# The copy of the value sums ahead of both feature activations on the scalar engine

## Chip, cores and metric

The kernel runs on one core of one Trainium2 chip. The metric is the device time of one execution in microseconds (us); the median of several runs counts. The engines are named as in the profile: PE multiplies matrices, DVE is the vector engine, ACT the scalar engine, POOL the third elementwise engine, SP issues the transfers.

## What is computed

Four layers follow each other on x of 2048 rows by 512 in float32: A, B, A, B with the same weights each time. Each adds its result to x after a layer norm. The change lies in layer B, an attention with a memory, over 32 heads of width 16, in 4 segments of 512 rows:

```python
phi = lambda t: jnp.where(t > 0, t + 1.0, jnp.exp(t))
for s in range(N):
    qs, ks, vs = q[:, :, s], k[:, :, s], v[:, :, s]
    logits = jnp.einsum("bhqd,bhkd->bhqk", qs, ks) * scale + mask
    p = _softmax(logits, axis=-1)
    a_dot = jnp.einsum("bhqk,bhkd->bhqd", p, vs)
    pq = phi(qs)
    num = jnp.einsum("bhld,bhde->bhle", pq, M)
    den = jnp.einsum("bhld,bhd->bhl", pq, z)[..., None] + 1e-6
    a_mem = num / den
    o = g * a_mem + (1.0 - g) * a_dot
    outs.append(o)
    pk = phi(ks)
    M = M + jnp.einsum("bhld,bhle->bhde", pk, vs)
    z = z + jnp.einsum("bhld->bhd", pk)
```

Layer A (a linear attention with learned features) is not touched by the change.

## The kernel before

Layer B works on groups m = 0 to 31: a segment s = m // 8, a block c of 8 heads, and half of that block, 4 heads. The class LayerB writes the whole order of work by hand in `steps` (line 865). Its loop (line 941) runs over k, five steps for each group. Below, "step 5.2 of segment 0" means local group 5, third of its five steps (k = 8*5*s + 5*5 + 2). In each step stand, in this order:

- `attend` (line 776): products of keys and queries into lg, of which there is one buffer. ACT takes the exponential, lg to P; POOL zeroes the masked part of P.
- `maxima` (line 735), nine steps ahead of `attend`: the same products into the buffer mx for a later group. DVE takes row maxima out of it into mxs.
- what an earlier step put off: first the `late` list (DVE differences), then the `later` list.
- `weighted` (line 812), at steps .0 and .2: the product of P and the values into pv, one buffer. The sums of group m are finished at step .2 of group m + 1, and there ACT copies pv, scaled by share, into U (line 836). U has two buffers.
- the work of a table (GAPS, line 43, and LAST for the last segment): steps .1, .3 and .4 have a cell each, such as

```
5.1 max q1+~       | 5.3 fin v0+/3     | 5.4 v0+ t3
6.1 max a0+ k1+~   | 6.3 a0+ fin v1+/3 | 6.4 v1+ m3 load
7.1 max n n q2+~   | 7.3 fin n v2+/3   | 7.4 v2+ t0+
```

In the cells q, k and v are projections of queries, keys and values (a + means for the next segment), out is the output projection, a the product of a query's features with the memory, t and m the memory's update, n and ln pieces of the next layer norm, max the negated maxima, and fin is `finish` (line 839): PE transposes U of the group before, and DVE divides the sums by their row sum (`weigh`, line 366; buffers r, ot, wt or tmp).

A projection ends in `proj` (line 654). ACT writes the high part of the product pp (a buffer of g) into a buffer ta1 or U. DVE writes the low part, the difference, which a ~ in the cell puts off to the next step by `late`. If the features phi are needed, two functions go into `later` and run in the next step:

```python
def first():
    act.activation(e, pp, AF.Exp)

def second():
    act.activation(r, pp, AF.Relu)
    pool.tensor_scalar(e, e, 1.0, None, op0=MIN)
    pool.tensor_tensor(out=e, in0=e, in1=r, op=ADD)
```

The profile calls e and r both tb. Projections with features end at .1 of groups 0, 1, 2, 4, 5, 6 and 7 of a segment, so their two functions run at step .2, where `weighted` also writes U. One a segment (q0+) ends at 3.4 and its functions run at 4.0, where `weighted` only adds products to pv.

PE is held in the order of the program (`held`, line 125). From k = 3 on so are DVE, ACT and POOL in layer B (`Ordered`, line 107), except that the exponential of lg and the maxima have high priority. The buffers of g are three, used in turn; a product into g waits until the third one before it has been read by all its readers.

The scheduling loop and what it calls, with line numbers:

Of the kernel before, what the change touches and what calls it, by code (L numbers as in the profile page):

```python
# [69 lines left out]
def interleave_kernel(ctx, tc, x_in, a_wqkv, a_wphi, a_wo, b_wq, b_wk, b_wv, b_wo, b_beta,  # L70
# [109 lines left out]
    def load_w(key, src=None, tag="w8"):  # L180
        w = []
        for _ in bring(w, key, src, tag):
            pass
        return w
# [16 lines left out]
    def settle():  # L201
        for k, t in owed:
            dma(k, t)
        owed.clear()
# [10 lines left out]
    def plain(src):  # L215
        def get(kc):
            raw = T2("x", 4)
            nc.sync.dma_start(out=raw, in_=src[kc * P : (kc + 1) * P, :])
            return raw
        return get  # L220
# [194 lines left out]
    def chain(*gens):  # L415
        for g in gens:
            yield from g
# [37 lines left out]
    class LayerA:  # L455
# [4 lines left out]
        def pass1(self, first):  # L460
# [19 lines left out]
            for s in range(NSEG):  # L480
# [46 lines left out]
                def go(steps):  # L527
                    for step in steps.split():
                        yield from {"k": kproj, "q": qproj, "v": kv}[step[0]](int(step[1]))
                        if step == "q0" and s == NSEG - 1:  # L530
                            self.e0 = self.feats(0)
# [10 lines left out]
                for _ in go(steps):  # L542
                    n += SIDE
                    while n >= 1:
                        n -= 1
                        next(side, None)
                    yield
# [60 lines left out]
    class LayerB:  # L608
# [256 lines left out]
        def steps(self, side, after):  # L865

            N = 8 * NSEG
            at = chain(*[self.attend(m) for m in range(N)])  # L870
            ma = chain(*[self.maxima(m) for m in range(N)])
            self.w4 = []
            self.wnext = [(m, c) for _ in range(NSEG) for c in range(NC) for m in range(2)]
            norms = [self.norm(0)]
            for _ in range(6):
                next(norms[0])
            self.wv = load_w("bwv", plain(b_wv))
            settle()
            for _ in range(2):
                self.queue_w()  # L880
            mem = {(s, c): self.memory(s, c) for s in range(NSEG) for c in range(NC)}
            val = [self.values(s) for s in range(NSEG)]
            outs, proj, part = {}, {}, {}
            weights = self.weights()

            def do(what, s, k):
                self.put_off = what[-1] == "~"
                what, _, quarters = what.rstrip("~").partition("/")
                s += what[-1] == "+"
                what = what.rstrip("+")  # L890
                i = int(what[-1]) if what[-1].isdigit() else None
                op = what.rstrip("0123456789")
                if op == "max":
                    if (k + LEAD) // R <= N:
                        self.put_maxima((k + LEAD) // R - 1)
                elif op == "fin":
                    if k >= FINAT:
                        self.finish((k - FINAT) // R)
                elif op in ("q", "k", "v", "out"):
                    if op == "out":  # L900
                        if s == 0:
                            return
                        g = outs[s]
                    elif op == "v":
                        g = after if i is None else val[s]
                    else:
                        g = proj.setdefault((s, i, op), self.proj(s, i, "qk".index(op)))
                    n = int(quarters) if quarters else 4 - part.pop(op, 0)
                    if quarters:
                        part[op] = n  # L910
                    for _ in range(n):
                        next(g, None)
                elif op == "load":
                    if s < NSEG - 2:
                        norms.append(self.norm(s + 2 if k > 0 else 1))
                        next(norms[-1])
                elif op == "n":
                    if s != NSEG - 2 or k % (8 * R) < 6 * R:
                        next(after if s == NSEG - 1 else norms[-1], None)
                elif op == "ln":  # L920
                    next(after if s == NSEG - 1 else norms[-1], None)
                elif op in ("a", "t", "m"):
                    if op != "a" or s > 0:
                        next(mem[s, i], None)
                elif s > 0:
                    if s not in outs:
                        outs[s] = self.out(s - 1)
                    next(outs[s])

            table = {k: (v.split(), 0) for k, v in BEFORE.items()}  # L930
            for s in range(NSEG):
                for cell in (GAPS if s < NSEG - 1 else LAST).replace("|", "\n").split("\n"):
                    if cell.strip():
                        at_, *what = cell.split()
                        m, j = at_.split(".")
                        if s == 0:
                            what = [w for w in what if not w.startswith("v3")]
                        table[8 * R * s + R * int(m) + int(j)] = what, s
            slots = [k for k in range(BEGIN, 2) if k < -LEAD or k % R in FILL]
            spent = 0.0  # L940
            for k in range(BEGIN, R * N + 4):
                strict[0] = True
                m = k // R + 3
                if k % R == 0 and 0 <= m < N:
                    self.stack(m)
                if 0 <= k < R * N:
                    next(at)
                if -LEAD <= k < R * N - LEAD:
                    next(ma)
                ordered[0] = ORDERED <= k < R * N  # L950
                late, self.late = self.late, []
                for f in late:
                    f()
                later, self.later = self.later, []
                for f in later[:1]:
                    f()
                if k % R in (0, 2) and 0 <= k // R - 1 < N:
                    self.weighted(k // R - 1, k % R == 2)
                for f in later[1:]:
                    f()  # L960
                if k in slots:
                    want = LEFT * (1 + slots.index(k)) / len(slots) if k < slots[-1] else 1e9
                    while spent + 100 < want:
                        before = work[0]
                        if next(side, None) is PAUSE:
                            break
                        spent += work[0] - before
                what, s = table.get(k, ((), 0))
                for w in what:
                    do(w, s, k)  # L970
                if 18 <= k < 28 and k % R in FILL:
                    next(weights, None)
            self.finish(N - 1)
            self.put_off = False
            for _ in self.out(NSEG - 1):
                pass
            strict[0] = ordered[0] = False
# [52 lines left out]
```

## Time and profile before

| | |
|---|---|
| median of 3 runs | 1740.95 us (1740.75 to 1749.43) |
| profiled execution | 1744.38 us, span 1742.4 us |
| granted PE clock, mean | 0.961 |
| busy: PE, DVE, ACT, POOL | 1552.9, 1183.8, 785.7, 544.0 us |
| DMA, mean | 111 GB/s |

The span is the time from the first to the last instruction of the profiled execution, which itself took a little longer. Engines overlap, so the busy times don't add up. A row of the order of time holds the start in us, the duration in us, the engine, the line, the operation, what it writes and reads, and in brackets the idle time of the engine before it with what ended it. A row of the waits holds who waited for whom, the total in us, how often, and the longest. All operations of ACT, DVE and POOL bear line 116, and those of PE lines 137 and 141, since helpers issue them; the names of the buffers tell them apart.

The layer B's groups run from about 399 to 800 us and from about 1248 to 1640 us of the span, with some more behind each.

### The profile page before, as it was taken

How to read it: one execution, taken by the hardware profiler on the slowest of the kernel's cores; microseconds unless marked ns; L12 is line 12 of the kernel's file. 1: busy time of each engine (PE TensorE's matmuls, PEld its weight loads, DVE VectorE, ACT ScalarE, POOL GpSimd, SP SyncE). 2: the span in 40 equal slices, each digit the busy share in tenths (PEclk: the TensorE clock that was granted, in tenths of full speed). 3: DMA queues.
4: the chain of work that ended last, by engine and by line, in shares of the span. 5: the costliest groups of instructions: out<-in, count | busy, mean ns of one | idle time of the engine just before them, and what ended most of it. 6: DMA issues, size and time to landing. Idle time of an engine off the chain costs nothing.

```text
span 1742.4 us, 28146 instructions
## 1 busy us (share of the span) xinstructions
PE 1552.9 (89%) x9856; PEld 1105.5 (63%) x9856; DVE 1183.8 (68%) x3358; ACT 785.7 (45%) x1202; POOL 544.0 (31%) x840
## 2 busy tenths in 40 slices
PE   5999898978899999998889998888889999999987
PEld 4888787755555555654568887776555565565544
DVE  4666785567778778778546677745677777776761
ACT  5433343225555555555533333422455555545542
POOL 2322431212433443332221233120244434433321
PEclk9999999989999999999999998899799999999997
DMA  9512345323534334345232025333443343343310
GB/s 333 201 49 85 94 138 185 117 74 89 179 84 132 96 91 133 94 146 140 80 107 76 25 93 162 110 109 109 123 116 92 98 127 99 86 122 80 98 44 31
DMA packets 99973, 193.67 MB, mean 111 GB/s; under 512 B 13432, under 2 KB 27000, under 8 KB 96760
## 3 DMA queue, kind: packets, MB, share of 16 engines
q1 hardware_dynamic: 98680, 191.35, 37.3%
q8 instruction: 79, 1.29, 0.3%
q10 hardware_dynamic: 1152, 0.52, 0.1%
q14 instruction: 62, 0.51, 0.1%
HBM read 96.86 MB, written 41.94 MB: 80 GB/s over the span
## 4 chain that ended last, share of the span: by engine, by line
PE 64%; DVE 18%; ACT 7%; DMA 6%; issue 4%; SPq 1%; POOL 1%; DVEq 0%; ACTq 0%; POOLq 0%
PE g L137 40%; DVE mx L116 9%; PE mx L137 7%; PE lg L137 7%; PE pv L137 5%; PE g L141 4%; ACT P L116 2%; DMA x<-x 2%; DVE mxs L116 2%; ACT U L116 1%; DMA tb<-pq 1%; DVE st L116 1%; ACT tb L116 1%; ACT x L116 1%; DVE ta L116 1%
## 5 line engine op out<-in xcount | busy, mean ns | idle before, releaser
L116 DVE CUSTOM_DVE_ANT_0 mx<-mx,mask 128x128 f32<-128x128 f32 (+3 forms) x1024 | 511.0, 499 | 227.1 <-PE mx L137 193.3
L116 ACT ACTIVATE P<-lg 128x1024 f32<-128x1024 f32 x320 | 328.8, 1027 | 250.6 <-PE lg L137 247.5
L116 POOL TENSOR_SCALAR_AFFINE_SELECT P<-P 128x256 f32<-128x256 f32 (+1 forms) x448 | 191.0, 440 | 550.9 <-ACT P L116 550.8
L137 PE MATMUL mx<-e,e 63*128 63x256 f32 (+2 forms) x1024 | 158.4, 367 | 60.7 <-DVE mxs L116 53.0
L137 PE MATMUL g<-w,oh 128*128 128x512 f32 x512 | 181.8, 438 | 9.3 <-ACT oh L116 5.4
L137 PE MATMUL lg<-e,e 64*128 64x256 f32 (+2 forms) x1024 | 171.7, 393 | 15.6 <-ACT P L116 14.3
L137 PE MATMUL g<-hh,wqk 128*128 128x512 f32 x512 | 179.2, 409 | 1.5 <-ACT mt L116 1.5
L137 PE MATMUL pv<-P,v 128*32 128x512 f32 (+3 forms) x2048 | 171.3, 454 | 0.1
L137 PE MATMUL g<-w,hh 128*128 128x512 f32 x512 | 168.2, 409 | 0.5 <-DVE e L116 0.5
L137 PEld LDWEIGHTS mx<-e,e 63*128 63x128 f32 x1024 | 85.2, 191 | 113.3 <-DVE mxs L116 87.8
L137 PEld LDWEIGHTS lg<-e,e 64*128 64x128 f32 x1024 | 83.0, 188 | 112.5 <-issue 58.1
L116 DVE DVE_READ_ACCUMULATOR2_ANT mxs<- 128x1 f32 x1024 | 144.8, 141 | 0.0
L116 POOL TENSOR_SCALAR tb<-tb 128x512 f32<-128x512 f32 x48 | 71.3, 1486 | 184.6 <-ACT tb L116 184.6
L137 PEld LDWEIGHTS pv<-P,v 128*32 128x32 f32 x2048 | 54.9, 112 | 103.5 <-issue 90.5
L137 PEld LDWEIGHTS g<-w,oh 128*128 128x128 f32 x512 | 97.1, 205 | 33.2 <-ACT oh L116 7.3
L137 PEld LDWEIGHTS g<-hh,wqk 128*128 128x128 f32 x512 | 98.1, 192 | 23.8 <-ACT mt L116 2.5
L137 PE MATMUL g<-w,ol 128*128 128x512 f32 x256 | 107.6, 420 | 0.8 <-DVE ol L116 0.8
L137 PEld LDWEIGHTS g<-w,hh 128*128 128x128 f32 x512 | 92.1, 191 | 20.8 <-DVE e L116 0.7
L137 PE MATMUL g<-w,hl 128*128 128x512 f32 x256 | 101.1, 395 | 0.0
L137 PE MATMUL g<-hl,wqk 128*128 128x512 f32 x256 | 101.0, 395 | 0.0
L116 DVE TENSOR_REDUCE es<-P 128x64 f32<-128x1024 f32 x64 | 76.6, 1197 | 34.8 <-ACT P L116 34.7
L137 PE MATMUL g<-w,e 128*128 128x512 f32 x384 | 97.7, 396 | 0.0
(117 smaller groups left out, 2547.6 us busy)
## 6 DMA issues: line engine op xcount, KB each, us to landing
e<-ta SPq DMA_DIRECT2D x264, 128.0 KB
wqk<-wqk SPq DMA_DIRECT2D x64, 512.0 KB
x<-x SPq DMA_DIRECT2D x48, 256.0 KB
e<-U SPq DMA_DIRECT2D x80, 128.0 KB
pq<-tb SPq DMA_DIRECT2D x32, 256.0 KB
tb<-pq SPq DMA_DIRECT2D x32, 256.0 KB
xr<-x SPq DMA_DIRECT2D x29, 256.0 KB
x<-in SPq DMA_DIRECT2D x28, 256.0 KB
```

What stands on the lines that cost most here:

```text
L116: i = f(*a, **k)
L137: return held(nc.tensor.matmul(*a, **k))
L141: return held(nc.tensor.transpose(*a))
```

## The change

Before, the first function of `later` ran ahead of `weighted` and the others behind it. Now all run behind it. On ACT at step .2 the order was: exponential, copy to U, second activation. It becomes: copy to U, exponential, second activation. POOL's two operations on the features are still issued right behind the second activation.

```diff
                 late, self.late = self.late, []
                 for f in late:
                     f()
-                later, self.later = self.later, []
-                for f in later[:1]:
-                    f()
                 if k % R in (0, 2) and 0 <= k // R - 1 < N:
                     self.weighted(k // R - 1, k % R == 2)
-                for f in later[1:]:
+                later, self.later = self.later, []
+                for f in later:
                     f()
```

## Prediction

> **What bounds the kernel now.** I read the page first, then the waits of the matrix engine in the two stretches of layer B (399 to 800 us and 1248 to 1640 us of the span), then the order of time of three engines around single copies U. The page says that PE leads but is not alone.
>
> ```profile
> span 1742.4 us, 28146 instructions
> PE 64%; DVE 18%; ACT 7%; DMA 6%; issue 4%; SPq 1%; POOL 1%; DVEq 0%; ACTq 0%; POOLq 0%
> 399.00:800.00 401.00, 366.40 (x2608) 231.95 (x2606) 305.51 (x1037) 214.98 (x308) 154.91 (x264) 0.99 0.43 118
> PE g L141 <- ACT U L116: 16.8, 18, 1.2
> ```
>
> The second line gives the chain that ended last; the third is the stretch of the first layer B (length, then busy time of PE, weight loads, DVE, ACT and POOL, granted clock, DMA share, GB/s): PE busy 366 of 401 us at a clock of 0.99, so its instructions run at nearly full speed and only its idle time can be had. The fourth line is the largest wait of PE in that stretch, and the view for the second layer B answers with the same line: 18 times PE stood before the transposes of U until ACT had written U, 33.6 us in both layers. Single ones are of two sizes, 1.19 and 0.53 us (rows of both below); 11 and 7 of them make 16.8.
>
> What makes U late is the row of time at one of these places (step 5.2 of the first segment; ACT, then PE, then DVE):
>
> ```profile
> 460.89 0.60 ACT L116 ACTIVATE tb<-g 128x512 f32<-128x512 f32 x1 [1.28 <-DVE ta L116]
> 461.39 0.68 ACT L116 ACTIVATE U<-pv,share 128x512 f32<-128x512 f32 x1
> 461.96 0.60 ACT L116 ACTIVATE tb<-g 128x512 f32<-128x512 f32 x1
> 462.43 1.04 ACT L116 ACTIVATE P<-lg 128x1024 f32<-128x1024 f32 x1
> 458.65 1.28 PE L137 MATMUL pv<-P,v 128*32 128x384 f32 x16
> 460.37 0.56 PE L137 MATMUL mx<-e,e 63*128 63x256 f32 x4
> 462.12 0.66 PE L141 MATMUL g<-ident,U 128*128 128x128 f32 x4 [1.19 <-ACT U L116]
> 462.53 0.72 PE L137 MATMUL g<-w,hh 128*128 128x512 f32 x2
> 464.81 0.50 PE L137 MATMUL lg<-e,e 64*128 64x256 f32 x4
> 460.18 0.69 DVE L116 TENSOR_TENSOR ta<-g,ta 128x512 fp32r<-128x512 f32 x1
> 463.19 0.42 DVE L116 TENSOR_TENSOR ot<-g,r 128x256 f32<-128x256 f32 x1
> 465.58 0.43 DVE L116 CUSTOM_DVE_ANT_0 mx<-mx,mask 128x256 f32<-128x256 f32 x1 [1.97 <-PE mx L137]
> ```
>
> The value sums pv are complete at 458.65 + 1.28 = 459.93. ACT idles 1.28 us, because the exponential at its head waits until DVE has formed the low part ta at about 460.87. Only then comes U, though its input has been there for a microsecond, and PE idles 1.19 us.
>
> Steps without features show the other order already, here step 3.2 of the second segment (ACT, then PE):
>
> ```profile
> 558.10 0.69 ACT L116 ACTIVATE U<-pv,share 128x512 f32<-128x512 f32 x1 [0.39 <-PE pv L137]
> 556.75 1.28 PE L137 MATMUL pv<-P,v 128*32 128x384 f32 x16
> 558.47 0.56 PE L137 MATMUL mx<-e,e 63*128 63x256 f32 x4
> 558.96 0.66 PE L141 MATMUL g<-ident,U 128*128 128x128 f32 x4
> ```
>
> U is released by pv alone, and the transposes start as the products mx end, with no idle time before them.
>
> **The change, part by part.** No operation is added or taken out. In the built order of the changed program, U stands ahead of the exponential at 36 places (18 a layer); PE, DVE and POOL keep their order. A layer has 24 such pairs of activations; around the other six (q0 of segments 1 to 3, which fall on step 4.0, and k0, k1, k2 of segment 0, which come before the first U) there is no U at that place, and nothing changes.
>
> *U itself.* At the place above it can start 0.07 us after pv (558.10 against 556.75 + 1.28 has the same distance), at 460.00, and be done at 460.68, before PE has finished mx at 460.93. The exponential doesn't move: its DVE wait ends at 460.87, and U, which takes 0.57 us of issue (461.39 to 461.96), frees the engine at 460.57. Margin 0.3 us. The second activation and P then come 0.57 us earlier, at 461.39 and 461.86. So U costs nothing where it goes: it lies in the 1.28 us hole.
>
> *What is late next* differs by the cell of the table. Four kinds:
>
> (a) Cells 5.3 and 7.3 of segments 0 to 2, and 1.3 of segment 3: no product with the memory stands between mx and the transposes, and PE can gain 1.19. The next lg would start at 463.62; P ends at 461.86 + 1.04 = 462.90, so it does not hold it. DVE is free from 463.61 and waits 1.97 us for PE. In 7.3 and in the first layer's last 1.3 DVE has less idle time left:
>
> ```profile
> 496.82 0.43 DVE L116 CUSTOM_DVE_ANT_0 mx<-mx,mask 128x256 f32<-128x256 f32 x1 [1.11 <-PE mx L137]
> 626.60 0.43 DVE L116 CUSTOM_DVE_ANT_0 mx<-mx,mask 128x256 f32<-128x256 f32 x1 [1.06 <-PE mx L137]
> 754.78 0.43 DVE L116 CUSTOM_DVE_ANT_0 mx<-mx,mask 128x256 f32<-128x256 f32 x1 [1.90 <-PE mx L137]
> 785.21 0.43 DVE L116 CUSTOM_DVE_ANT_0 mx<-mx,mask 128x256 f32<-128x256 f32 x1 [1.07 <-PE mx L137]
> 1633.08 0.43 DVE L116 CUSTOM_DVE_ANT_0 mx<-mx,mask 128x256 f32<-128x256 f32 x1 [1.89 <-PE mx L137]
> ```
>
> So per layer 3 x 1.19 for 5.3, 1.11 + 1.06 + 1.19 for 7.3, and 1.07 in segment 3 of the first layer or 1.19 in the second (the row at 1633.08: no next layer's norm on DVE there): 8.0 and 8.1 us.
>
> (b) Cells 0.3 (segments 1, 2), 6.3 (0, 1) and 4.3 (1): the memory products run first, PE waits less, and the product that follows the transposes gets the third buffer of g, the one that the second activation reads:
>
> ```profile
> 477.80 0.60 ACT L116 ACTIVATE tb<-g 128x512 f32<-128x512 f32 x1
> 477.96 0.66 PE L141 MATMUL g<-ident,U 128*128 128x128 f32 x4 [0.53 <-ACT U L116]
> 478.45 0.73 PE L137 MATMUL g<-w,hh 128*128 128x512 f32 x2
> 481.49 0.43 DVE L116 CUSTOM_DVE_ANT_0 mx<-mx,mask 128x256 f32<-128x256 f32 x1 [1.21 <-PE mx L137]
> ```
>
> The product starts 0.49 us after the transposes, not 0.41 as in (a): at 478.45, just as the second activation ends at 478.40. That activation comes 0.57 us earlier, and DVE has 1.21 us to spare: 5 x 0.57 = 2.85 us a layer.
>
> (c) Cells 2.3 and 4.3 of segment 0: the next lg waits for P, which moves by 0.57 us.
>
> ```profile
> 418.73 0.50 PE L137 MATMUL lg<-e,e 64*128 64x256 f32 x4 [0.30 <-ACT P L116]
> 448.85 0.80 PE L137 MATMUL lg<-e,e 64*128 64x256 f32 x4 [0.74 <-ACT P L116]
> 449.33 0.97 DVE L116 TENSOR_TENSOR w<-x,w 128x512 fp32r<-128x512 f32 x1 [0.40 <-ACT w L116]
> ```
>
> In the first layer's 4.3 DVE has only 0.40 us before it is the limit. 0.97 us in the first layer, 1.14 in the second.
>
> (d) Cells 1.3 and 2.3 of segments 1 and 2: nothing. There DVE ends last and does not wait for U:
>
> ```profile
> 524.93 0.66 PE L141 MATMUL g<-ident,U 128*128 128x128 f32 x4 [1.19 <-ACT U L116]
> 528.80 0.42 DVE L116 CUSTOM_DVE_ANT_0 mx<-mx,mask 128x256 f32<-128x256 f32 x1
> 530.92 0.49 PE L137 MATMUL mx<-e,e 63*128 63x512 f32 x2 [0.39 <-DVE mxs L116]
> 541.17 0.66 PE L141 MATMUL g<-ident,U 128*128 128x128 f32 x4 [0.53 <-ACT U L116]
> 543.02 0.71 PE L137 MATMUL g<-w,oh 128*128 128x512 f32 x2 [0.70 <-DVE tmp L116]
> ```
>
> At 528.80 DVE comes to the maxima without any idle time, from the norm's small operations, and PE waits for it at 530.92; at 543.02 the product waits for the memory's quotient tmp. The transposes come earlier and the time is waited out there.
>
> Sum: 8.0 + 2.85 + 0.97 = 11.8 and 8.1 + 2.85 + 1.14 = 12.1, together 24 us of the 33.6.
>
> *Queues moved past.* POOL's minimum needs only the exponential, which stays. On SP one stack transfer goes ahead of a write of x at four places:
>
> ```profile
> 532.74 0.54 SPq L362 DMA_DIRECT2D x<-mmq x1
> 533.33 0.53 SPq L144 DMA_DIRECT2D e<-ta x1
> ```
>
> Either gains or loses about 0.55 us of issue, several steps before its reader: taken as nothing, at the most 4 x 0.55 = 2.2 us either way.
>
> *Does the gain stay?* After each place PE, DVE and ACT only wait for each other, so the rest moves along, unless a transfer doesn't. The chain of the first stretch has one that ended last:
>
> ```profile
> 772.66 7.11 DMA e<-U
> ```
>
> It is issued and used between two copies, so I expect it to move along. The chains of both layers hold such transfers at four places; lost there, 4 x 1.19 = 4.8 us would go.
>
> **A rule against the change.** At 460.89 ACT does nothing but wait, with a U behind it that could run: in this trace a waiting head holds the rest. The Trainium skill, "PSUM — Partial Sum Buffer", section "Engine vs sequencer instructions", says that ScalarE's queue is strictly first in, first out. By that rule, with which the trace agrees, the changed order can lose in the same way: a U whose pv comes late would hold both activations and P. That is the slower rival below.
>
> **The rivals.**
>
> *Half of it (0.16).* Everywhere the second activation and P decide, not U, so that each place of (a), (b) and (c) gets 0.55 us: 28 x 0.55 = 15 us, 1726. For it: that is so in (b) and (c). Against it: 0.72 us between P's end (462.90) and the lg that needs it (463.62) in (a).
>
> *The time is given back (0.08).* DVE, at 305 of 401 us, or a transfer sets the pace of a group over its five steps, and (d) is the rule: 0 to 8.7 us, about 1737. Against it: the idle times of DVE shown in (a) and (b). That the change doesn't do what it says is excluded by the built order.
>
> *A late U holds ACT (0.05), slower.* Place: the head of ACT at step 2. U now waits for the last pv, which needs POOL's mask on P and v, and, in the built program, at 6 of the 36 places for the transfer that reads its old buffer. It decides from 0.3 us of lateness, when the exponential slips; from 0.3 + 0.57 = 0.87 the second activation is later than now, and (b) and (c) turn to a loss. At 1.15 us in all 36 places it costs about 36 x 0.28 = 10 us: 1751. Against it: pv ended 0.96 us before the exponential in the rows above, and U ran 0.07 us after pv at 558.10.
>
> *All of it (0.03).* All 33.6 us: 1707.
>
> **How the numbers follow.** The profiled execution took 1744.38 us (span 1742.4 and 2 us around it): I expect 1720 for such a one. It lies 3.4 us above the median of 1740.95, from which the forecast is 1740.95 - 24 = 1717 us, with a chance of 0.68. Its own range is 1712 (29 us: the four DVE-bound places in (d) at the long wait give 4 x 1.19 more) to 1722 (the four transfers). 8 times in 10: from 1707 (all the waits of PE for U) to 1730 (half of it, with the 2.2 us on SP and two of the four transfers, 2.4 us, lost as well). A run of this kernel tells 0.5%, 8.7 us, from no change. Faster by more: forecast, half and all, 0.87; within: 0.08; slower by more: 0.05.
>
> **What would show it.** Right: PE's wait for U gone in both stretches; U released by pv in the 36 places, 0.07 us behind; the exponential still released by DVE; lg in 4.3 of segment 0 still waiting for P; PE's wait for DVE's mxs up by about what (d) loses, some 5 us. Each layer B about 12 us shorter, the rest of the span unchanged. Wrong: ACT's U waiting for POOL's mask or a DMA with PE's wait for P up (a late U), or the idle of DVE in (a) and (b) not falling while PE waits for transfers (given back).

## Result and profile after

The changed kernel took 1720.89 us (median of 4 runs, 1717.88 to 1726.66) against 1741.59 us (4 runs) for the kernel before on the same chip: ratio 0.9875, 95% interval 0.9834 to 0.9916, some 22 us less by the ratio. Its profiled execution took 1723.36 us. The page's span and the shares of its chain; then the stretches of both layers B (columns as before); then PE's longest wait in the first of them:

```profile
span 1721.4 us, 28141 instructions
...
PE 69%; DVE 17%; ACT 5%; DMA 4%; issue 3%; SPq 1%; POOL 0%; POOLq 0%; ACTq 0%; DVEq 0%
```

```profile
399.00:800.00 401.00, 373.50 (x2662) 234.96 (x2662) 314.83 (x1067) 222.67 (x318) 157.63 (x270) 0.98 0.44 121
1248.00:1640.00 392.00, 371.23 (x2653) 233.49 (x2651) 303.37 (x1029) 217.22 (x307) 155.34 (x266) 0.98 0.39 103
```

```profile
PE mx L137 <- DVE mxs L116: 15.9, 21, 2.3
```

The line of U, 16.8 us and first in this list before, is gone from both stretches; PE is busy 373.5 of 401 us instead of 366.4. What leads now is the wait for DVE's maxima, 10.8 us in this stretch before, and 59.2 against 53.0 us in the whole span.

The order of time at the place that the prediction showed, step 5.2 of the first segment:

```profile
460.34 0.69 ACT L116 ACTIVATE U<-pv,share 128x512 f32<-128x512 f32 x1 [0.38 <-PE pv L137]
461.23 1.09 ACT L116 ACTIVATE tb<-g 128x512 f32<-128x512 f32 x2 [0.20 <-DVE ta L116]
462.20 1.04 ACT L116 ACTIVATE P<-lg 128x1024 f32<-128x1024 f32 x1
458.99 1.28 PE L137 MATMUL pv<-P,v 128*32 128x384 f32 x16
460.71 0.56 PE L137 MATMUL mx<-e,e 63*128 63x256 f32 x4
461.19 0.66 PE L141 MATMUL g<-ident,U 128*128 128x128 f32 x4
463.86 0.50 PE L137 MATMUL lg<-e,e 64*128 64x256 f32 x4
464.64 0.43 DVE L116 CUSTOM_DVE_ANT_0 mx<-mx,mask 128x256 f32<-128x256 f32 x1 [0.69 <-PE mx L137]
```

U starts 0.07 us behind pv (458.99 + 1.28 = 460.27), the exponential still waits for DVE, and the transposes follow mx without a pause. The first two hold at all 36 places of this trace; in the kernel before, U started 1.45 us behind pv at 35 of them. P ends at 463.24, ahead of the lg at 463.86. DVE's idle time fell from 1.97 to 0.69 us: the 1.28 us that PE won here came out of it.

To see how much each layer gained, here are the transposes of one U near the start and one near the end of each layer B, first of the kernel before, then of the changed one:

```profile
399.01 0.66 PE L141 MATMUL g<-ident,U 128*128 128x128 f32 x4
796.90 0.60 PE L141 MATMUL g<-ident,U 128*128 128x128 f32 x4
1248.85 0.66 PE L141 MATMUL g<-ident,U 128*128 128x128 f32 x4
1644.76 0.60 PE L141 MATMUL g<-ident,U 128*128 128x128 f32 x4
```

```profile
398.33 0.65 PE L141 MATMUL g<-ident,U 128*128 128x128 f32 x4
786.51 0.60 PE L141 MATMUL g<-ident,U 128*128 128x128 f32 x4
1241.32 0.66 PE L141 MATMUL g<-ident,U 128*128 128x128 f32 x4
1625.53 0.60 PE L141 MATMUL g<-ident,U 128*128 128x128 f32 x4
```

The first layer is 397.89 - 388.18 = 9.7 us shorter, the second 395.91 - 384.21 = 11.7. Between them 2.9 us were given back. Most of that way is layer A, where the order of PE, DVE and POOL is that of before; the granted clock was 0.91 in a stretch of 100 us (990 to 1090) that showed 0.95 before (1000 to 1100). Below, "the two layers" means these two distances against the kernel before.

### The profile page after: what moved, and what is told of

It reads as the page before. It is cut to its first block, busy times and chain, and to the rows that moved or that the text cites. A ratio compares the mean times of both kernels' runs of the same rounds, so it can differ in the third digit from the quotient of the medians.

```text
span 1721.4 us, 28141 instructions
## 1 busy us (share of the span) xinstructions
PE 1552.4 (90%) x9856; PEld 1105.7 (64%) x9856; DVE 1184.7 (69%) x3358; ACT 791.5 (46%) x1202; POOL 543.8 (32%) x840
## 4 chain that ended last, share of the span: by engine, by line
PE 69%; DVE 17%; ACT 5%; DMA 4%; issue 3%; SPq 1%; POOL 0%; POOLq 0%; ACTq 0%; DVEq 0%
PE g L137 41%; DVE mx L116 8%; PE mx L137 8%; PE lg L137 8%; PE pv L137 7%; PE g L141 4%; ACT P L116 2%; DMA x<-x 1%; DVE mxs L116 1%; DVE st L116 1%; ACT x L116 1%; DVE es L116 1%; DMA tb<-pq 1%; DVE P L116 1%; DVE bs L116 1%
## 5 line engine op out<-in xcount | busy, mean ns | idle before, releaser
L137 PE MATMUL mx<-e,e 63*128 63x256 f32 (+2 forms) x1024 | 158.6, 367 | 67.0 <-DVE mxs L116 59.2
L137 PE MATMUL lg<-e,e 64*128 64x256 f32 (+2 forms) x1024 | 171.3, 392 | 18.7 <-ACT P L116 17.3
```

What stands on the lines that cost most here:

```text
L137: return held(nc.tensor.matmul(*a, **k))
```

## Experiments

**One kind at a time.** `place` is the prediction's kind of a step .2; the new order holds only where the letter is listed. The edit shown is the one for kind (a), against the kernel before.

```diff
+                g, s = k // R % 8, k // (8 * R)
+                place = ("d" if g in (1, 2) and s in (1, 2) else "a" if g in (5, 7) or (g, s) == (1, 3) else
+                         "c" if s == 0 and g in (2, 4) else "b")
                 later, self.later = self.later, []
-                for f in later[:1]:
+                head = 0 if place in "a" else 1
+                for f in later[:head]:
                     f()
...
-                for f in later[1:]:
+                for f in later[head:]:
```

The changed kernel again, on the same chip as the three partial ones.

> The changed kernel itself, timed beside the three partial versions on one chip. The wait-for-U theory (time is won only where the transposes of U ended a wait of PE): 18 to 24 us under the kernel before, places (a) 1.25 us each, (b) 0.57, (c) 0.57 or less, (d) nothing or a small loss. The half theory (the second activation and P decide everywhere): 14 x 2 x 0.55 = 15 us. Its single run before lost 0.4 us at each 1.3 of segments 1 and 2 where nothing was expected; if that is no accident it is here again.

Kind (a) alone.

> The new order only at the 14 places (a): cells 5.3 and 7.3 of segments 0 to 2 and 1.3 of segment 3. Wait-for-U: 14 x 1.25 less what DVE keeps in 7.3 (4 x 0.1) = 17 us under the kernel before. Half: 14 x 0.57 = 8 us. Given back evenly over the groups: 14/36 of the whole gain of 21, 8 us.

Kind (d) alone.

> The new order only at the 8 places (d): cells 1.3 and 2.3 of segments 1 and 2. Wait-for-U with DVE as the limit there: 0 us, or up to 3 us slower (0.4 us at each 1.3, and a lower clock after the longer pause of PE); PE's wait for U is gone there, and the wait of the product mx for DVE grows from 0.4 to 2.0 us. Given back evenly: 8/36 of 21, 5 us faster. Half: 4 us faster.

Kinds (a), (b) and (c).

> The new order at the 28 places (a), (b) and (c), the old one at (d). Wait-for-U: 22 to 25 us under the kernel before, that is as fast as the full change or up to 3 us faster. Given back evenly: 28/36 of 21 = 16 us, 5 us slower than the full change.

| new order at | ratio to before, 95% | the two layers, us |
|---|---|---|
| all (the change) | 0.9868 (0.9838 to 0.9898) | -10.0, -12.1 |
| (a) | 0.9912 (0.9879 to 0.9944) | -8.7, -8.6 |
| (a), (b), (c) | 0.9869 (0.9844 to 0.9894) | -10.6, -12.9 |
| (d) | 1.0046 (1.0025 to 1.0067) | +1.2, +1.9 |

Kind (a) alone brings 17.3 us in the two layers and 15 us in the time (0.0088 x 1743): the prediction's 16, and twice what "half of it" allows (14 x 0.55 = 7.7). Kinds (b) and (c) add 1.9 and 4.3 us. Kind (d) adds nothing; it costs a little, and its own run was 8 us slower than before, more than its two layers explain.

**Kind (d) in the last layer B alone,** to see whether those 8 us belong to (d): `head = 0 if self.last and g in (1, 2) and s in (1, 2) else 1`. With (d) in both layers, DVE's operations in the second layer A, whose order is not held by the program, also come in another order than before; here they do not.

> The new order only at kind (d), cells 1.3 and 2.3 of segments 1 and 2, and only in the last layer B; the first layer B keeps the old one, and so does the plan of the second layer A (DVE's order in it is that of the kernel before; in the run with kind (d) in both layers B it differed at five stretches). Theory: the 9 us that kind (d) cost beyond its own places came from that other plan of the second layer A, so that here 0.5 to 2 us are lost, each place 1.3 some 0.4 and by chance one slow stretch of PE's clock more. Rival: the new order at (d) itself costs 4 us or more a layer, and here 4 us or more are lost.

Ratio 1.0023 (1.0004 to 1.0043), 4 us slower. Its last layer B is 2.5 us longer, of which 2.0 lie at the (d) places; its untouched first layer B differs by 0.1. But the way from the first layer B to the second, with the plan of before, came out 5.3 us longer too, against 9.4 us with (d) in both layers; in the run with (a) alone, which has that other order of DVE as well, it was 1.5 us shorter. So (d) itself costs 1 to 2 us a layer (some 0.4 at each of its two segments, and 1.2 more where a slow stretch of PE, in which products take about twice as long, falls behind it). The time is what the rival gave, 4 us, but its 4 us at the places of (d) are not there. That the other order in layer A cost the rest of the 8 us is not shown either: this stays open.

**Both activations ahead of U,** so that U is the last of the three:

```diff
+                later, self.later = self.later, []
+                for f in later:
+                    f()
                 if k % R in (0, 2) and 0 <= k // R - 1 < N:
                     self.weighted(k // R - 1, k % R == 2)
-                later, self.later = self.later, []
-                for f in later:
-                    f()
```

> Both activations of the features go ahead of U (exponential, second activation, U), so that U still stands behind the waiting exponential and comes 0.47 us later than in the kernel before, while the second activation comes 0.57 us earlier and P at the same time. Theory (U decides in kinds (a) and (b)): every place of (a) loses 0.47 (14 places, 6.6 us), every place of (b) too (10 places, 4.7 us), (c) about nothing since its product waits for P anyway: about 11 us slower than before, with PE's wait for U up from 36 to 50 us or more. Rival, half of it (the second activation and P decide everywhere): (b) gains up to 0.5 us a place, 5 us faster than before, or no change. The plan of the second layer A changes in this build at some places of DVE, so that the two layers B are read by themselves.

Ratio 1.0142 (1.0108 to 1.0177), 25 us slower; the two layers +14.4 and +16.0. The sign is the theory's and "half of it" is out; the loss, though, is more than twice as large as expected. The order of PE's time at a place of kind (a) shows why:

```profile
495.31 0.66 PE L141 MATMUL g<-ident,U 128*128 128x128 f32 x4 [1.68 <-ACT U L116]
495.72 1.02 PE L137 MATMUL g<-w,hh 128*128 128x512 f32 x2
496.53 0.63 PE L137 MATMUL g<-w,hl 128*128 128x512 f32 x1
496.96 1.06 PE L137 MATMUL g<-w,hh 128*128 128x512 f32 x2
497.81 0.63 PE L137 MATMUL g<-w,hl 128*128 128x512 f32 x1
498.24 1.06 PE L137 MATMUL g<-w,hh 128*128 128x512 f32 x2
...
500.77 0.39 PE L137 MATMUL g<-w,hl 128*128 128x512 f32 x1
```

The pause grew by 0.49 us as expected (1.68 instead of 1.19). Behind it the same product takes 0.63 instead of 0.39 us for nearly 4 us, and the next transposes come 1.6 us later than behind a like pause without this. Counted by the rows of these products, that is so behind 13 of the 18 pauses of 1.68 us at the places of (a) and in 1.3 of segments 1 and 2. Nine of them, at (a), cost 1.5 to 1.6 us each, and four, in 1.3, about 1.1: some 18 of the 19 us that the expectation missed.

**Pauses of set length.** In the kernel before, copies of 128x128 of a constant were put between the exponential and U at kind (a), as many as the segment's number (0 to 3):

```diff
+                g, s = k // R % 8, k // (8 * R)
+                if later and k % R == 2 and (g in (5, 7) or (g, s) == (1, 3)):
+                    for _ in range(s):
+                        act.activation(spare_out, mask[:, 0:P], AF.Identity, scale=share[:, 0:1])
```

> The kernel before, with copies of 128x128 of a constant (0.40 us of issue each) between the exponential and U at the places of kind (a): none in segment 0, one in segment 1, two in segment 2, three in segment 3, so that PE's pause for U is 1.19, 1.59, 1.99 and 2.39 us (4, 4, 4 and 2 places). Theory (a pause beyond some 1.4 us can make the granted clock fall for about 3.4 us, as at 12 of 16 pauses of 1.68 us): after 1.19 no product is slowed; after 1.59 about half; after 1.99 and 2.39 three quarters or more, each with 1.3 to 1.5 us more than the pause itself; the four places without slowing end in another phase of a grid of 3.41 us than the others. In all 4 x 0.40 + 4 x 0.80 + 2 x 1.20 = 7.2 us of pauses and some 8 x 1.4 = 11 us of slow stretches. Rival (a pause costs its length and no more): 7 us, products at full speed behind every pause.

Ratio 1.0087 (1.0048 to 1.0126), 15 us slower. PE's pauses came out as 1.19, 1.48, 1.91 and 2.34 us. The expectation's 12 of 16 are 13 of 18 by the count above. Slowed were none behind 1.19, 1 of 4 behind 1.48, 0 of 4 behind 1.91 and 1 of 2 behind 2.34: slow stretches are there again, but their share does not grow with the length as expected. The two layers are +3.2 and +6.2: 4 x 0.29 + 4 x 0.72 + 2 x 1.15 = 6.3 us of longer pauses and two slow stretches of about 1.5. The rest lies outside them: in the profiled execution 5.9 us ahead of the first layer B and 2.6 behind the second. Its cause is not shown. A pause of each sort:

```profile
728.21 0.66 PE L141 MATMUL g<-ident,U 128*128 128x128 f32 x4 [1.92 <-ACT U L116]
728.62 0.70 PE L137 MATMUL g<-w,hh 128*128 128x512 f32 x2
729.16 0.40 PE L137 MATMUL g<-w,hl 128*128 128x512 f32 x1
...
1447.53 0.78 PE L141 MATMUL g<-ident,U 128*128 128x128 f32 x4 [1.48 <-ACT U L116]
1447.97 1.20 PE L137 MATMUL g<-w,hh 128*128 128x512 f32 x2
1448.97 0.63 PE L137 MATMUL g<-w,hl 128*128 128x512 f32 x1
```

What parts them may be when the pause ends, on a grid of 3.4133 us (last section); this was read out of the traces, and no run set the phase.

**U early, P as late as before.** Two such copies behind the second activation:

```diff
                 for f in later:
                     f()
+                if later and k % R == 2:
+                    for _ in range(2):
+                        act.activation(spare_out, mask[:, 0:P], AF.Identity, scale=share[:, 0:1])
```

> The new order, with two copies of 128x128 of a constant (0.28 us of issue each, an estimate from U's 0.57 for 384 columns) put behind the second activation at each of the places, so that P and the next copies come as late as in the kernel before, while U and both activations stay as early as in the changed kernel. Theory: U decides in (a) and (b), but in (a) P at its old time (its end at 462.90 against a product that could start at 462.37) lets only 0.72 of the 1.25 us through; (b) keeps its 0.57; (c) loses all. So about 14 x 0.53 + 2 = 9 us of the gain go: about 12 us faster than before. Rival, half of it (P decides everywhere): nothing is left, within 3 us of before. Third reading (P has no share in (a)): 2 us slower than the changed kernel, 19 us faster than before. The plan of the second layer A changes in this build at some places of DVE, so that the two layers B are read by themselves.

Ratio 0.9927 (0.99 to 0.9953), 13 us faster than before, as expected in the time but not in the working. The two layers are -8.3 and -8.0. At step 5.2:

```profile
462.61 1.01 ACT L116 ACTIVATE P<-lg 128x1024 f32<-128x1024 f32 x1
463.67 0.50 PE L137 MATMUL lg<-e,e 64*128 64x256 f32 x4
```

P ends at 463.62, which is 0.15 us later even than in the kernel before (463.47, with pv at the same 458.65), and lg follows 0.05 us later. By the shift of the next transposes this costs about 0.13 of the 1.25 us at a place of kind (a), not the 0.53 expected; the rest of what is missing is (c), as expected, and a slow stretch behind 1.3 of the second segment in each layer. "Half of it" wanted nothing to be left: U's own time brings most of the gain in (a), and all of it in (b), with P held at its old one.

**A later U.** Four such copies ahead of U, in the new order:

```diff
+                later, self.later = self.later, []
+                if later and k % R == 2:
+                    for _ in range(4):
+                        act.activation(spare_out, mask[:, 0:P], AF.Identity, scale=share[:, 0:1])
                 if k % R in (0, 2) and 0 <= k // R - 1 < N:
                     self.weighted(k // R - 1, k % R == 2)
-                later, self.later = self.later, []
                 for f in later:
```

> The new order, with four copies of 128x128 of a constant (0.28 us of issue each, an estimate) ahead of U, which comes 0.73 us later than in the changed kernel: ACT is free 0.32 us before pv is complete. The exponential then starts 0.43 us later than in the kernel before, the second activation 0.15 us earlier. Theory: (a) keeps 0.75 of its 1.25 us (14 places, 10.5 us), (b) and (c) 0.1 to 0.15 each (1.5 to 2 us): about 12 us faster than before, 9 us slower than the changed kernel; (d) costs what it costs there. Rival, half of it (only the second activation and P decide): 0.15 us at 28 places, 4 us faster than before.

Ratio 0.9994 (0.9976 to 1.0012), no change; the two layers are -1.2 and -1.0. The expectation fell by the size of the copies, and the trace shows it (ACT, then PE):

```profile
464.75 1.70 ACT L116 ACTIVATE spare_out<-mask,share 128x128 f32<-128x128 f32 x4
466.36 0.67 ACT L116 ACTIVATE U<-pv,share 128x512 f32<-128x512 f32 x1
466.93 1.07 ACT L116 ACTIVATE tb<-g 128x512 f32<-128x512 f32 x2
463.89 1.28 PE L137 MATMUL pv<-P,v 128*32 128x384 f32 x16
467.08 0.66 PE L141 MATMUL g<-ident,U 128*128 128x128 f32 x4 [0.92 <-ACT U L116]
```

A copy takes 0.40 us of ACT (1.61 for four), not 0.28. So U starts 1.19 us behind pv (465.17), 1.12 later than in the changed kernel and 0.27 earlier than in the kernel before, and PE waits 0.92 instead of 1.19. With these numbers the theory gives 14 x 0.27 = 3.8 us won in (a) and, the second activation and P being 0.2 us later than before, 14 x 0.2 = 2.8 lost in (b) and (c): 1 us faster; 2.1 were measured in the layers. A version meant to put U later still, with three copies of 128x512, did not fit into memory and has no time.

**Away with the next wait.** In the changed kernel PE now waits at 2.3 of segments 1 and 2 for DVE's tmp, as the prediction's kind (d) had it; the table's cell was edited:

```diff
-2.1 max a2 n n k3~ | 2.3 a2 fin n ln out/3 | 2.4 out ln m1 turn~
+2.1 max a2 n n k3~ | 2.3 a2 fin n out/3 ln | 2.4 out ln m1 turn~
```

> The changed kernel, with one cell of the table edited: in cell 2.3 the transposes of the layer norm (ln) stand behind the output projection (out/3) and not ahead of it. In the changed kernel PE waits 1.27 us at four places (cell 2.3 of segments 1 and 2) until DVE has read the memory product's buffer (tmp), because the output projection gets that buffer; now it gets the one before, which is free, and the transposes take the late one. Theory: the wait at 2.3 was all that kept the new order from gaining there, so 0.9 to 1.27 us at each of the four places, 3.6 to 5 us faster than the changed kernel, 0.9845 of the kernel before. Rival: DVE, which is late in these steps anyhow (it comes to the maxima without idle time), sets the pace, the wait moves to mxs in the next cell, and nothing is gained.

PE at 2.3 of the second segment, in the changed kernel:

```profile
537.55 0.60 PE L141 MATMUL g<-ident,U 128*128 128x128 f32 x4
538.15 0.66 PE L141 MATMUL g<-ident,x 128*128 128x128 f32 x4
540.08 0.71 PE L137 MATMUL g<-w,oh 128*128 128x512 f32 x2 [1.27 <-DVE tmp L116]
```

and with the cell edited:

```profile
537.27 0.60 PE L141 MATMUL g<-ident,U 128*128 128x128 f32 x4
537.88 0.74 PE L137 MATMUL g<-w,oh 128*128 128x512 f32 x2
```

The wait is gone, and the next transposes of U come 0.9 us earlier against the changed kernel at each place. The two layers are -10.6 and -12.7 against -10.0 and -12.1, with one slow stretch of 1.2 us in each that the changed kernel did not have there. The time is 0.9876 of before (0.9842 to 0.991): the 4 x 0.9 us are in the trace, but no gain over the changed kernel can be told in the time. It is the fastest profiled execution (span 1714.4 us), not a proven better version.

## Why the prediction was right

The forecast of 24 us less and the ratio's 21.8 (14.6 to 28.9) agree; the time, 1720.89 us, lies inside the range, 3.9 us above the 1717 forecast. The mechanism agrees too. By its steps:

- *U costs nothing in the hole.* Held: 0.07 us behind pv, the exponential released by DVE as before. It starts 0.20 us after U's end, and 0.32 us after the 0.57 us of issue by which the prediction had worked out a margin of 0.3.
- *(a), 16.1 us.* Held: 17.3 in the layers with (a) alone. Single places gave 1.25, not 1.19: the transposes also came nearer to mx. In 7.3 DVE took back up to 0.1, less than its shorter idle time said.
- *(b) and (c), 7.8 us.* 6.2 in the layers. By the run with (a), (b) and (c) against the one with (a) alone, single places of (b) gave 0.52 to 0.62 for the 0.57 forecast, 5.7 us together: this term was right. The term of (c) was too large: some 0.4 us came of the 2.1. The wait for P in 4.3 of segment 0 stayed, as said; but what had been two pauses there is one of 1.43 us now, and in the first layer products were slow behind it from about 448.3 to 455.0 us, 6.7 us, where before it was 3.3. That took the gain of this cell and 1.5 us more. The product pv, 1.28 us long before, shows it in the changed kernel:

```profile
447.14 0.50 PE L137 MATMUL lg<-e,e 64*128 64x256 f32 x4 [1.43 <-ACT P L116]
451.91 2.36 PE L137 MATMUL pv<-P,v 128*32 128x512 f32 x16
```

- *(d), nothing.* Too good by 1 to 2 us a layer. 2.3 gave exactly nothing. In 1.3 some 0.38 us were lost, which no step had: the small operations of the norm on DVE now meet POOL's mask (last section).
- *PE's wait for mxs up by 5.* 6.2.
- *Each layer B 12 us shorter, the rest unchanged.* 9.7 and 11.7 in one execution, 10.0 and 12.1 in the other. The rest was not unchanged: the way between the two layers was 2.9 us longer in the one execution and 0.2 shorter in the other, in the same kernel.

Of the rivals, "half of it" fell three times: by (a) alone, with both activations ahead of U, and with P held back. "Given back" is true of (d), as forecast, and of 4.3 of segment 0 in the first layer. The price of "a late U" was mis-sized: it gave 36 x 0.28 = 10 us lost at a lateness of 1.15 us, by the second activation alone. At 1.12 us nothing was lost, because U still came 0.27 us earlier than behind the exponential, and (a), which has 14 of the 28 places that pay, goes by U. Of the Trainium skill's first-in, first-out rule ("PSUM — Partial Sum Buffer", section "Engine vs sequencer instructions") the trace agrees: the exponential, waiting for DVE, held U before. That a U waiting for its pv would hold both activations in the same way is not shown; in the run with a later U they were late because copies ran ahead of it.

## What to carry to other kernels

Where an engine that works in order has a waiting instruction at its head, look behind it for one whose input is already there; if that one fits into the hole (here 0.57 us of issue in 1.28), moving it up need cost nothing. The gain is then the idle time of whoever waits for it, place by place, less what the next engine in line (here DVE) has to give, and nothing where that engine is last already. A pause of PE may cost more than its length, so compare kernels by the time between the same instructions in the changed stretch, not by the span alone.

## What was not expected of the hardware

**A pause of PE of under 2 us can halve its rate for some 3.5 us.** Groups of three products that start every 0.69 us started every 1.28 us (496.96 to 498.24 in the rows of both activations ahead of U). It happened behind none of the 96 pauses of 0.9 to 1.3 us for U in the layers B of all these executions, segment 0's cells 2.3 and 4.3 left out, but behind 13 of 18 of 1.68 us. In 4.3 of segment 0 a second pause, of 0.74 us for P, follows, and there products were slow in the first layer of the kernel before too. Taken modulo 3.4133 us, the 13 end between 3.32 and 0.98 (round the end of the grid), the other 5 between 1.63 and 3.19. In the run with set pauses, on what looks like the same phase, the two slowed ones end at 0.28 and 3.34, and those of 1.91 us and more that were not slowed between 1.17 and 2.52; but one of 1.48 us that ended at 0.91 was not slowed. The Trainium skill, "TensorE: Matmul & The Clock Gate", section "Part 1: The HAM clock gate (the "warmup" mystery)", has a free-running window of 3413 ns after which the rate is halved or restored. The length of the grid above is taken from there; the phases and the halved rate agree with it, but no run here measures the length by itself. The same page of the Trainium skill, section "HAM oscillation — how this bites in real kernels", puts the danger at idle gaps above 3.4 us; here 1.68 us were enough. What share of a window must be idle is left open.

**POOL can stretch a small operation of DVE.** The last two-input operation of the norm in 1.3 of segments 1 and 2, in the kernel with (a), (b), (c) alone, then in the changed kernel with the POOL operation beside it:

```profile
527.69 0.17 DVE L116 SCALAR_TENSOR_TENSOR st<-st 128x4 f32<-128x4 f32 x1
```

```profile
525.30 0.64 POOL L116 TENSOR_SCALAR_AFFINE_SELECT P<-P 128x512 f32<-128x512 f32 x1
525.41 0.55 DVE L116 SCALAR_TENSOR_TENSOR st<-st 128x4 f32<-128x4 f32 x1
```

It takes 0.55 instead of 0.17 us at all four places, and ends as POOL's mask ends (525.94). P comes earlier there and brings the mask forward onto it. This is no accident of these places: in all traces of this case, the 50 such operations that run beside one of POOL are stretched, and the 142 that don't are not; each stretched one ends within 0.03 us of the end of a POOL operation. The Trainium skill, "GPSIMD Engine Reference", section "1. Specifications", says that POOL shares its memory interfaces with DVE, with contention for DVE's instructions with two inputs there; the rows agree. In the forecast, (d) was free because DVE had no idle time there; that DVE's own work could grow was missed.
